# Hashed attention and a maxout feed-forward layer on one core: where operands are transposed, when weights are loaded, and how feed-forward work is spread over attention steps

## The chip, the cores and the metric

The kernel runs on one core of one Trainium2 chip. Its time is device time in microseconds (us) of one execution. Five engines take part, each working through its own instructions in order: PE (matmuls; PEld are its weight loads), DVE and ACT (element-wise work, the only two here that read PSUM), POOL (element-wise work in SBUF, and the issuing of most loads) and SP (only the issuing of transfers).

## The reference

```python
q_bits = (np.einsum('bhsd,dk->bhsk', q, proj) > 0).astype(np.int64)
k_bits = (np.einsum('bhsd,dk->bhsk', k, proj) > 0).astype(np.int64)
q_bucket = np.sum(q_bits * powers, axis=-1)      # powers = 1, 2, 4, ... 32
k_bucket = np.sum(k_bits * powers, axis=-1)
mask = q_bucket[:, :, :, None] == k_bucket[:, :, None, :]
scores = np.where(mask, scale * np.matmul(q, k.transpose(0, 1, 3, 2)), -1000000000.0)
attn = softmax(scores)                           # a row without a match becomes uniform
attn_out = np.matmul(attn, v)
x = attn_out.transpose(0, 2, 1, 3).reshape(B * S, H * D)
h = np.maximum(np.maximum(x @ w1, x @ w2), x @ w3)
out = h @ w_out
```

q, k and v are 4 x 8 x 768 x 64 (batch, heads, sequence, head size), proj is 64 x 6, w1 to w3 are 512 x 768, w_out is 768 x 512, the output 3072 x 512, all float32.

## The kernel before

**Attention.** Heads go in pairs: 4 batches of 4 pairs. For each pair, q and k are loaded as float32, split on DVE into an fp16 head (`tensor_scalar`, line 121) and an fp16 residual (line 122), and the result is transposed (line 125) by a DMA that SP issues, into `qT` and `kT` with 128 rows: 64 of heads, 64 of residuals. The hash is a matmul of all 128 rows with the projection (line 133, into `hps`, two halves of eight matmuls); DVE compares with zero (lines 144 and 150, `hb`) and writes six rows of plus or minus a constant over the first residual rows (line 154). Score matmuls then use 70 rows: scores plus a number that is largest where all six bits agree, so that the exponential of anything else vanishes. `vcast` makes fp16 v with a column of ones in `vone`; `meanv` gives the mean of v (`svp`, `mv`) for rows without a match.

**Units.** A unit is two blocks of 128 keys against 384 queries: 2 matmuls (line 186, `sc`), one ACT exponential of 128 x 768 (line 190, `AT`), 6 matmuls with v (line 206, `av`). There are 192 units: 4 batches, 2 halves of the queries, 4 pairs, 2 heads, 3 units. After the six units of a pair and half, `norm` divides by the sum (DVE lines 221, 223, 228; POOL 224, 225, 230) into `xn`.

**Feed-forward.** After the four pairs of a half batch, `xn` (384 tokens x 512) is transposed by one DMA that SP issues (line 233, `xT`). `push_ffn` appends 21 pieces called atoms: 18 first-layer atoms of 4 matmuls (line 246, `ps`; the first of three is copied by ACT on line 251, the others are maxed in by DVE on line 253, `ht`) with a cost of 0.64, and 3 output atoms of 6 matmuls (line 258, `po`; copied to `osb` by DVE or ACT, stored by SP) with a cost of 1.28.

**Order.** The order on every engine is that of the code. One step of the main loop issues the scores of unit u, the v matmuls of unit u-2, what the table `todo` holds for step u (loads, splits, hashes, means, put there by `at(step, ...)`), and atoms. From step 32 on each step adds a rate of about 0.76 to a credit, whether atoms are there or not, and issues atoms while the credit allows. Hashes, means and atoms share the PSUM pool `mm_ps`, which has two buffers.

**Loads.** The first q, k and v are issued by SP; the weights are four whole loads on POOL at steps 0, 1, 3 and 8; pairs of later batches are loaded by POOL 6 steps ahead of their split, and hashed 6 and 7 steps behind it, one pair every 5 steps.

Of the kernel before, what the change touches and what calls it, by code (L numbers as in the profile page):

```python
# [7 lines left out]

# [7 lines left out]
def kernel(  # L16
# [30 lines left out]
    TINY = 1e-30  # L47
# [39 lines left out]
    nc.vector.memset(bias_t[:], EXP_BIAS)  # L87
    ones = konst.tile([P, P], FP16, name="ones")
# [13 lines left out]
    nc.vector.tensor_copy(ph[:], p32[:])  # L102
# [7 lines left out]
    def load_w(i):  # L110
        w_ap = (moe_w1, moe_w2, moe_w3)[i]
        nc.gpsimd.dma_start(w_sb[i][:], w_ap.rearrange("(c p) f -> p c f", p=P))


    T = {}

    def split(b, pr):
        for n in "qk":
            x32 = raws.pop((n, b, pr))[:].rearrange("p h (c d) -> p (h c) d", d=D)
            s = spl.tile([P, 2 * NCH, 2 * D], FP16, tag=n + "s", name=n + "s")  # L120
# [7 lines left out]
    def hash_mm(b, pr, half):  # L128
        hps = mm_ps.tile([P, 512], FP32, tag="mm", name="hps")
        c0 = half * CH  # L130
        for s, w in ((True, PA), (False, PB)):
            for g, (n, hh) in enumerate((("q", 0), ("k", 0), ("q", 1), ("k", 1))):
                nc.tensor.matmul(hps[32 * g : 32 * (g + 1), 0:HQ], w[:],  # L133
                                 T[n, b, pr][:, hh * NCH + c0 : hh * NCH + c0 + CH, :],
                                 start=s, stop=not s)
        return hps

    hbs = {}

    def hash_a(b, pr):  # L140
# [190 lines left out]
    for u in range(N + LAG):  # L331
        if u < N:
            score(u)
        if u >= LAG:
            attend(u - LAG)
# [40 lines left out]
```

## Time and profile before

| | |
|---|---|
| median of 3 runs | 429.3 us (427.68 to 432.57) |
| profiled execution | 430.04 us |
| its span, first to last instruction | 428.2 us |
| busy in the span: PE, DVE, ACT, POOL | 301.5, 197.3, 190.2, 113.5 us |
| mean granted TensorE clock | 0.86 |

In the profile's rows a group reads: line, engine, operation, output <- inputs with the program's names, count, busy time and mean ns; behind the bar the idle time just before these instructions and what ended most of it. A row of the waits reads: who waited, for whom, us in total, times, longest. A row of the timeline reads: start, duration (us), engine, line and operation. The granted clock is a share of full speed.

### The profile page before, as it was taken

To read this page: it belongs to the slowest core of one execution; us is meant where nothing else is said; L and a number is where in the kernel's file an instruction comes from. 1 tells how busy PE (TensorE), PEld (TensorE's weight loads), DVE (VectorE), ACT (ScalarE), POOL (GpSimd) and SP (SyncE) were. 2 spreads that over 40 slices of the span, in tenths; PEclk is the share of its full clock that TensorE was granted. 3 is DMA by queue.
4 is the path that set the end of the run, shared out by engine and by line. 5 is a ranking of instruction groups with operands and counts; after the bars stand their busy time and mean duration, and the time that the engine had idled before them with its cause. 6 is when DMAs were issued, how large, how long until landed. Compare 5 with 4: busy or idle time off the path is not lost.

```text
span 428.2 us, 6629 instructions
## 1 busy us (share of the span) xinstructions
PE 301.5 (70%) x2608; PEld 174.0 (41%) x2608; DVE 197.3 (46%) x394; ACT 190.2 (44%) x249; POOL 113.5 (26%) x159
## 2 busy tenths in 40 slices
PE   0406785887979916886589915979649983998396
PEld 0103443453546613543346502545325552555152
DVE  4506538586525522977424431686614320431043
ACT  1204456352667723543527820445331693159210
POOL 1501249331113640421301670043210141004200
PEclk9999658596999976989979965998758997999689
DMA  7996957973030493473110594147510101010201
GB/s 239 244 222 142 149 148 182 214 196 73 2 110 2 138 287 93 100 159 100 57 29 2 184 219 112 35 112 187 75 37 0 51 26 37 2 73 3 38 0 73
DMA packets 75551, 44.47 MB, mean 104 GB/s; under 512 B 64096, under 2 KB 69328, under 8 KB 75520
## 3 DMA queue, kind: packets, MB, share of 16 engines
q1 hardware_dynamic: 68624, 25.57, 27.0%
q0 software_dynamic: 6736, 18.48, 16.2%
q8 instruction: 20, 0.33, 0.3%
q14 instruction: 11, 0.09, 0.1%
q10 hardware_dynamic: 160, 0.00, 0.0%
HBM read 25.17 MB, written 6.29 MB: 73 GB/s over the span
## 4 chain that ended last, share of the span: by engine, by line
PE 47%; DMA 21%; DVE 13%; ACT 8%; issue 4%; POOL 3%; SPq 2%; POOLq 0%; ACTq 0%; DVEq 0%
PE ps L246 24%; DMA kT<-ks 11%; PE sc L186 9%; DMA xT<-xn 8%; ACT AT L190 8%; PE po L258 6%; PE av L206 4%; PE hps L133 3%; DVE qs L122 3%; SPq L125 2%; DVE qs L121 2%; DVE ks L121 2%; DVE ht L253 1%; DMA v<-in_v_dram 1%; POOL xn L230 1%
## 5 line engine op out<-in xcount | busy, mean ns | idle before, releaser
L190 ACT ACTIVATE AT<-sc,bias_t 128x768 f16<-128x768 f32 x192 | 165.2, 908 | 117.6 <-PE sc L186 116.6
L246 PE MATMUL ps<-xT,w_sb 128*128 128x384 f16 x576 | 125.4, 361 | 54.9 <-DMA xT<-xn 52.9
L186 PE MATMUL sc<-qT,kT 70*128 70x384 f16 x384 | 104.7, 358 | 9.4 <-ACT AT L190 2.3
L253 DVE TENSOR_TENSOR ht<-ht,ps 128x384 f16<-128x384 f16 x96 | 53.1, 553 | 117.0 <-PE ps L246 114.1
L246 PEld LDWEIGHTS <-w_sb 128*128 128x128 f16 x576 | 56.8, 106 | 103.2 <-issue 67.7
L206 PEld LDWEIGHTS <-AT 128*128 128x128 f16 x1152 | 66.7, 103 | 32.4 <-issue 10.3
L224 POOL TENSOR_SCALAR m<-dd 128x6 f32<-128x6 f32 x32 | 7.1, 223 | 264.3 <-DVE dd L221 264.2
L206 PE MATMUL av<-vone,AT 128*128 128x65 f16 x1152 | 72.1, 201 | 0.6 <-ACT AT L190 0.4
L251 ACT CAST ht<-ps 128x384 f16<-128x384 f32 x48 | 22.9, 476 | 103.0 <-PE ps L246 103.0
L186 PEld LDWEIGHTS <-kT 70*128 70x128 f16 x384 | 36.3, 103 | 37.6 <-issue 22.3
L133 PE MATMUL hps<-qT,PA 128*32 128x384 f16 x64 | 16.5, 400 | 47.9 <-DMA qT<-qs 35.2
L258 PE MATMUL po<-wout_sb,ht 128*128 128x512 f16 x144 | 35.6, 385 | 0.5 <-DVE ht L253 0.4
L230 POOL TENSOR_TENSOR xn<-xn,t 128x384 f16<-128x384 f16 x32 | 30.5, 952 | 2.5
L133 PEld LDWEIGHTS <-PA 128*32 128x32 f16 x128 | 5.2, 98 | 60.2 <-issue 47.0
L225 POOL TENSOR_TENSOR t<-m,mv 128x384 f32<-128x384 f32 x32 | 26.5, 828 | 2.7
L221 DVE TENSOR_SCALAR dd<-av 128x6 f32<-128x6 f32 x32 | 5.2, 163 | 39.0 <-PE av L206 38.8
L144 DVE TENSOR_SCALAR hb<-hps 128x384 f16<-128x384 f32 x16 | 8.8, 551 | 29.9 <-PE hps L133 29.9
L159 POOL CAST vone<-v 128x768 f16<-128x768 f32 x16 | 17.7, 1104 | 16.7 <-DMA v<-in_v_dram 16.5
L264 DVE COPY osb<-po 128x512 f32<-128x512 f32 x16 | 11.0, 690 | 22.9 <-PE po L258 22.9
L122 DVE SCALAR_TENSOR_TENSOR qs<-q,qs 128x768 f16<-128x768 f32 x16 | 20.4, 1277 | 0.5
L258 PEld LDWEIGHTS <-ht 128*128 128x128 f16 x144 | 12.9, 99 | 14.4 <-issue 1.8
L133 PE MATMUL hps<-kT,PA 128*32 128x384 f16 x64 | 13.1, 399 | 7.8 <-DMA kT<-ks 7.8
(34 smaller groups left out, 192.2 us busy)
## 6 DMA issues: line engine op xcount, KB each, us to landing
out_dram<-osb SPq DMA_DIRECT2D x24, 256.0 KB, 2.0
v<-in_v_dram POOLq DMA_DIRECT2D x15, 384.0 KB, 6.7
q<-in_q_dram POOLq DMA_DIRECT2D x12, 384.0 KB, 3.9
k<-in_k_dram POOLq DMA_DIRECT2D x12, 384.0 KB, 5.3
w_sb<-in_moe_w_dram POOLq DMA_DIRECT2D x3, 768.0 KB, 12.8
q<-in_q_dram SPq DMA_DIRECT2D x4, 384.0 KB, 4.1
k<-in_k_dram SPq DMA_DIRECT2D x4, 384.0 KB, 6.0
wout_sb<-in_moe_w_out_dram POOLq DMA_DIRECT2D x1, 768.0 KB, 8.5
```

What stands on the lines that cost most here:

```text
L122: nc.vector.scalar_tensor_tensor(out=s[:, :, D : 2 * D], in0=x32, scalar=QS, in1=s[:, :, 0:D], op0=AluOp.mult, op1=AluOp.subtract)
L133: nc.tensor.matmul(hps[32 * g : 32 * (g + 1), 0:HQ], w[:], T[n, b, pr][:, hh * NCH + c0 : hh * NCH + c0 + CH, :], start=s, stop=not s)
L159: nc.gpsimd.tensor_copy(vones[b % 2][:, 2 * pr : 2 * pr + 2, :, 0:D], v32)
L186: nc.tensor.matmul(sc[:, i, 0:HQ], kT[0:KR, hh * NCH + 2 * j + i, :], qT[0:KR, hh * NCH + hf * CH : hh * NCH + (hf + 1) * CH, :], start=Tr ...
L190: nc.scalar.activation(AT[:], sc[:, :, 0:HQ], ActFn.Exp, bias=bias_t[:], scale=EXP_SCALE)
L206: nc.tensor.matmul(av[:, o : o + D + 1], AT[:, i, c * P : (c + 1) * P], vones[b % 2][:, 2 * pr + hh, 2 * j + i, 0 : D + 1], start=first, s ...
L225: nc.gpsimd.tensor_tensor(out=t[:], in0=m[:].to_broadcast([P, 2, CH, D]), in1=mvs[b, pr][:].unsqueeze(2).to_broadcast([P, 2, CH, D]), op=A ...
L230: nc.gpsimd.tensor_tensor(out=xv, in0=xv, in1=t[:], op=AluOp.add)
L246: nc.tensor.matmul(ps[:, 0:HQ], w_sb[i][:, jc, fb * P : (fb + 1) * P], xT[:, :, jc, :], start=jc == 0, stop=jc == NJ - 1)
L251: nc.scalar.copy(ht[:], ps[:, 0:HQ])
L253: nc.vector.tensor_tensor(out=hts[fb][:], in0=hts[fb][:], in1=ps[:, 0:HQ], op=AluOp.max)
L258: nc.tensor.matmul(ps[:], hts[fb][:, c * P : (c + 1) * P], wout_sb[:, fb, :], start=fb == 0, stop=fb == NF - 1)
```

## The change

1. **First pair.** Its q and k are loaded head by head, q by SP and k by ACT. The heads are split on DVE and ACT, and transposed on PE: `pe_T` issues six 128 x 128 transposes into a PSUM tile, `evac_T` copies it to `qT` or `kT` by DVE (q) or ACT (k). `hash_head` hashes one head at a time. The projection operands are made behind the first copy (`make_p`).
2. **Second pair.** Its halves are split by POOL and DVE, and transposed on PE as well, at step 2 (`second`).
3. **x.** After every pair `x_T` transposes its 384 x 128 part of x on PE, five steps after the pair's last unit; DVE copies it into `xT`. No DMA transposes x any more.
4. **Other pairs** are still transposed by DMA, 9 or 10 steps ahead of their hash, with loads 10 steps ahead of the split, one pair every 6 steps (second batch) or 10 (third and fourth).
5. **Weights** w1 to w3 are loaded in halves of their columns at steps 6, 7, 9, 12, 13, 14, w_out at step 18.
6. **Pace.** A step adds 0.64 to the credit, and only while atoms are there; 21 atoms cost 24 x 0.64, and a half batch has 24 units.
7. **Normalisation.** The mean of v, now with the column of ones and times 1e-30, is added to numerator and denominator, then one reciprocal and one product (POOL, or DVE for the last pair) follow.

The core of the diff:

```diff
-    load_qk(0, 0, nc.sync)
-    load_qk(0, 1, nc.sync)
-    load_v(0, 0, nc.sync)
+    load("q", 0, 0, nc.sync, (1, 2))
+    load("k", 0, 0, nc.scalar, (1, 2))
+    load("q", 0, 1, nc.sync)
+    load("k", 0, 1, nc.sync)
+    load("v", 0, 0, nc.gpsimd)
...
+    def pe_T(n, b, pr, hh, tag):
+        pool = av_ps if tag == "av" else mm_ps
+        ps = pool.tile([P, 512], FP32, tag=tag, name="tps")
+        p16 = ps[:].bitcast(FP16)
+        for c in range(NCH):
+            nc.tensor.transpose(p16[:, c * P : (c + 1) * P], S16[n, b, pr][:, hh * NCH + c, :], iden[:])
+        return p16
...
+    def hash_head(b, pr, hh):
+        tq, tk = T["q", b, pr], T["k", b, pr]
+        hb = small.tile([P, S], FP16, tag="hb", name="hb")
+        hps = hash_mm([(tk, hh, 0), (tq, hh, 0), (tk, hh, 1), (tq, hh, 1)])
+        hash_cmp(hb[:, 0:HQ], hps)
+        for g, (t, half) in enumerate(((tk, 0), (tq, 0), (tk, 1), (tq, 1))):
+            a = hh * NCH + half * CH
+            hash_row(t[D : D + NBITS, a : a + CH, :].rearrange("p a t -> p (a t)"),
+                     hb[32 * g : 32 * g + NBITS, 0:HQ])
...
             norm(b, hf, pr)
+            at(u + LAG + 3, lambda: x_T(b, hf, pr))
...
+        nc.vector.tensor_tensor(out=t[:, :, :, 0 : D + 1], in0=av[:, :, :, 0 : D + 1],
+                                in1=mvs[b, pr][:].unsqueeze(2).to_broadcast([P, 2, CH, D + 1]),
+                                op=AluOp.add)
+        nc.vector.reciprocal(rr[:], t[:, :, :, D : D + 1])
+        eng = nc.vector if pr == NP - 1 else nc.gpsimd
+        eng.tensor_tensor(out=xv, in0=t[:, :, :, 0:D], in1=rr[:].to_broadcast([P, 2, CH, D]),
+                          op=AluOp.mult)
+
+    def x_T(b, hf, pr):
         if pr == 0:
-            xns[b, hf] = xp.tile([P, CH, DM], FP16, tag="xn", name="xn")
...
+            xTs[b, hf] = xp.tile([P, NJ, HQ], FP16, tag="xT", name="xT")
+        xn = xns.pop((b, hf, pr))
+        ps = mm_ps.tile([P, 512], FP32, tag="mm", name="xps")
+        p16 = ps[:].bitcast(FP16)
+        for c in range(CH):
+            nc.tensor.transpose(p16[:, c * P : (c + 1) * P], xn[:, c, :], iden[:])
+        nc.vector.tensor_copy(xTs[b, hf][:, pr, :], p16[:, 0:HQ])
         if pr == NP - 1:
-            xT = xp.tile([P, CH, NJ, P], FP16, tag="xT", name="xT")
-            nc.sync.dma_start_transpose(xT[:].rearrange("p c j t -> p (c j) t"),
-                                        xns.pop((b, hf))[:].rearrange("p c m -> p (c m)"))
-            push_ffn(b, hf, xT)
+            push_ffn(b, hf, xTs.pop((b, hf)))
...
+    at(0, first_b)
+    at(1, lambda: split_r("q", 0, 1))
+    at(1, lambda: split_r("k", 0, 1))
+    at(2, second)
...
+    at(4, lambda: third(2))
+    at(6, lambda: load_w(0, 0))
+    at(8, lambda: third(3))
+    at(10, lambda: hash_half(0, 2, 0))
+    at(15, lambda: hash_half(0, 3, 0))
...
+    def prep(b, pr, s, lead, lag):
+        at(s - lead, lambda: [load(n, b, pr, nc.gpsimd) for n in "qkv"])
...
+        at(s, split)
+        at(s + 2, lambda: vcast(b, pr))
+        at(s + lag, lambda: hash_half(b, pr, 0))
+        at(s + lag + 1, lambda: hash_half(b, pr, 1))
+        at(s + lag + 1, lambda: hash_rows(b, pr))
+        at(s + lag + 2, lambda: meanv(b, pr))
...
+            if b == 1:
+                prep(b, pr, 32 + 6 * pr, 10, 9)
+            else:
+                prep(b, pr, 2 * (b - 1) * NUG + 14 + 10 * pr, 10, 10)
...
-        if u >= first and u < N:
-            credit += rate
+        if atoms:
+            credit += 0.64
```

(`first_b` and `second` call `pe_T` and `evac_T` for the second head of the first pair and for the second pair; `third` splits a pair and issues its DMA transposes.)

On SP, from the program's start, the issues before were these (loads of the first batch, with the transposes of the first two pairs between them; the names are the tiles written and read):

```order
L71 DMA q_99<-in_q_dram 128x2x384
L71 DMA k_101<-in_k_dram 128x2x384
L71 DMA q_103<-in_q_dram 128x2x384
L71 DMA k_105<-in_k_dram 128x2x384
L76 DMA v_107<-in_v_dram 128x2x384
L125 DMA_TRANSPOSE qT<-qs 128x12x128
L125 DMA_TRANSPOSE kT<-ks 128x12x128
L71 DMA q_141<-in_q_dram 128x2x384
L71 DMA k_143<-in_k_dram 128x2x384
L125 DMA_TRANSPOSE qT<-qs 128x12x128
L125 DMA_TRANSPOSE kT<-ks 128x12x128
```

In the changed kernel SP starts with these:

```order
L78 DMA q_96<-in_q_dram 128x384 x2
L78 DMA q_105<-in_q_dram 128x2x384
L78 DMA k_107<-in_k_dram 128x2x384
L78 DMA q_184<-in_q_dram 128x2x384
L78 DMA k_186<-in_k_dram 128x2x384
L78 DMA q_240<-in_q_dram 128x2x384
L78 DMA k_242<-in_k_dram 128x2x384
L152 DMA_TRANSPOSE qT<-qs 128x12x128
L152 DMA_TRANSPOSE kT<-ks 128x12x128
```

The four transposes of the first two pairs are gone, and the first one left (the third pair's) stands behind all q and k loads of the first batch.

On PE, where the feed-forward work of the first half batch begins, the rows before were these (the last matmuls of a mean, then the first atom, which reads the `xT` that a DMA writes):

```order
L166 LDWEIGHTS ones
L166 MATMUL svp<-vone_115,ones 128x128
L246 LDWEIGHTS w_sb
L246 MATMUL ps<-xT,w_sb 128x384
L246 LDWEIGHTS w_sb
L246 MATMUL ps<-xT,w_sb 128x384
```

In the changed kernel the same place reads (last matmul with v, three transposes of the last pair's part of x, first atom):

```order
L261 MATMUL av<-vone_122,AT 128x65
L292 LDWEIGHTS xn
L292 MATMUL xps<-iden,xn 128x128
L292 LDWEIGHTS xn
L292 MATMUL xps<-iden,xn 128x128
L292 LDWEIGHTS xn
L292 MATMUL xps<-iden,xn 128x128
L306 LDWEIGHTS w_sb
L306 MATMUL ps<-xT,w_sb 128x384
```

PE now makes the transposed x itself, in the rows right ahead of the atom that needs its copy.

On DVE, where a pair of a later batch is split (heads and residuals of q and k) while the pair before it is hashed (`hb` are the two compares, then four writes of rows), the rows before were these:

```order
L121 TENSOR_SCALAR qs<-q_1967 128x12x64
L122 SCALAR_TENSOR_TENSOR qs<-q_1967,qs 128x12x64
L121 TENSOR_SCALAR ks<-k_1969 128x12x64
L122 SCALAR_TENSOR_TENSOR ks<-k_1969,ks 128x12x64
L144 TENSOR_SCALAR hb<-hps 128x384
L253 TENSOR_TENSOR ht<-ht,ps 128x384
L150 TENSOR_SCALAR hb<-hps 128x384
L154 TENSOR_SCALAR qT<-hb 6x768
```

In the changed kernel a pair of the third batch:

```order
L179 TENSOR_SCALAR hb<-hps 128x384
L142 TENSOR_SCALAR qs<-q_1853 128x12x64
L148 SCALAR_TENSOR_TENSOR qs<-q_1853,qs 128x12x64
L142 TENSOR_SCALAR ks<-k_1855 128x12x64
L148 SCALAR_TENSOR_TENSOR ks<-k_1855,ks 128x12x64
L293 COPY xT<-xps 128x384
L313 TENSOR_TENSOR ht<-ht,ps 128x384
L179 TENSOR_SCALAR hb<-hps 128x384
L183 TENSOR_SCALAR qT<-hb 6x768
```

The first compare has moved ahead of the split; the second stays behind it, now with a copy of x between. In the second batch of the changed kernel split and hash of different pairs lie three steps apart.

More of the change, by code (lines that the diff above doesn't have):

```diff
@@ L129, in hash_mm @@
+    def hash_mm(groups):
         hps = mm_ps.tile([P, 512], FP32, tag="mm", name="hps")
[L130 removed]
         for s, w in ((True, PA), (False, PB)):
[L132 to L134 removed]
+            for g, (t, hh, half) in enumerate(groups):
+                a = hh * NCH + half * CH
+                nc.tensor.matmul(hps[32 * g : 32 * (g + 1), 0:HQ], w[:], t[:, a : a + CH, :],
@@ L148, in hash_b, with hash_row, hash_half, hash_rows @@
+    def hash_row(dst, src):
+        nc.vector.tensor_scalar(out=dst, in0=src, scalar1=2 * BIT, scalar2=None, op0=AluOp.mult)
+    hbs = {}
+    def hash_half(b, pr, half):
+        if half == 0:
+            hbs[b, pr] = small.tile([P, S], FP16, tag="hb", name="hb")
+        tq, tk = T["q", b, pr], T["k", b, pr]
+        hps = hash_mm([(tq, 0, half), (tk, 0, half), (tq, 1, half), (tk, 1, half)])
+        hash_cmp(hbs[b, pr][:, half * HQ : (half + 1) * HQ], hps)
+    def hash_rows(b, pr):
         hb = hbs.pop((b, pr))
-        hps = hash_mm(b, pr, 1)
@@ new lines, with first_b, second @@
+    hash_head(0, 0, 0)
+    split_r("k", 0, 0, (1, 2))
+    vcast(0, 0)
+    for n in "qk":
+        load(n, 0, 2, nc.sync)
+    load("v", 0, 1, nc.gpsimd)
+    operands(0, 1)
+    split_h("q", 0, 1, nc.gpsimd)
+    split_h("k", 0, 1, nc.gpsimd)
+    def first_b():
+        pq = pe_T("q", 0, 0, 1, "mm")
+        pk = pe_T("k", 0, 0, 1, "mm")
+        evac_T(pq, "q", 0, 0, 1, nc.vector)
+        evac_T(pk, "k", 0, 0, 1, nc.scalar)
+        hash_head(0, 0, 1)
+    def second():
+        for n in "qk":
+            for hh in range(2):
+                ps = pe_T(n, 0, 1, hh, "mm")
+                evac_T(ps, n, 0, 1, hh, nc.vector if n == "q" else nc.scalar)
@@ new lines, in third @@
+    def third(pr):
+        operands(0, pr)
+        for n in "qk":
+            split_h(n, 0, pr, nc.gpsimd if pr == 2 else nc.vector)
+            split_r(n, 0, pr)
+            xbar(n, 0, pr)
+    at(0, first_b)
+    at(0, lambda: vcast(0, 1))
+    at(1, lambda: split_r("q", 0, 1))
+    at(1, lambda: split_r("k", 0, 1))
+    at(2, second)
+    at(1, lambda: [load(n, 0, 3, nc.sync) for n in "qk"])
+    at(1, lambda: load("v", 0, 2, nc.gpsimd))
+    at(3, lambda: load("v", 0, 3, nc.gpsimd))
+    at(3, lambda: hash_half(0, 1, 0))
@@ L326 @@
     N = len(units)
-    total = 2 * B * (18 * 0.64 + 3 * 1.28)
-    first = NUG + 8
-    rate = total / (N - first + 2)
     credit = 0.0
-    for u in range(N + LAG):
+    for u in range(N + LAG + 4):
         if u < N:
             score(u)
-        if u >= LAG:
+        if LAG <= u < N + LAG:
             attend(u - LAG)
```

208 lines of the change are left out of this document (109 added, 99 removed).

## The prediction

> **What bounds the kernel now.** I cut the span at four places of the program: the first score matmul, step 32 (the first feed-forward matmul stands there), the last score step, the end. The table of windows gives each engine's busy time (with its count of instructions), the granted TensorE clock, the DMA share and GB/s; two later windows lie where operands for the next batch are made.
>
> ```profile
> 0.00:16.60 16.60, 1.94 (x16) 0.69 (x16) 9.76 (x22) 1.28 (x1) 6.90 (x12) 1.00 0.88 232
> 16.60:81.60 65.00, 37.40 (x339) 21.60 (x340) 29.44 (x59) 26.62 (x32) 19.43 (x26) 0.80 0.86 184
> 81.60:398.30 316.70, 242.50 (x2164) 142.18 (x2164) 149.18 (x296) 158.88 (x210) 85.17 (x118) 0.87 0.35 87
> 398.30:428.20 29.90, 19.69 (x90) 9.52 (x89) 8.94 (x17) 3.45 (x7) 1.97 (x3) 0.81 0.14 40
> 170.00:210.00 40.00, 32.60 (x333) 19.04 (x331) 31.26 (x60) 20.92 (x28) 10.81 (x14) 0.96 0.45 110
> 270.00:310.00 40.00, 31.03 (x308) 17.62 (x307) 29.69 (x57) 18.98 (x24) 10.81 (x14) 0.89 0.51 110
> ```
>
> The first column of busy time is PE. It works 37.4 of 65.0 us in the second stage, while DMA is at 0.86 of its engines; in the third it works 242.5 of 316.7, with every other engine half idle and DMA at 0.35. So the question is what PE, which takes its instructions in order, waits for. The first row below is from the waits of the whole span, the other two from the third stage alone (us in total, times, longest).
>
> ```profile
> PE hps L133 <- DMA qT<-qs: 35.2, 6, 13.2
> ...
> PE ps L246 <- DMA xT<-xn: 46.7, 6, 13.7
> PE hps L133 <- DVE hb L144: 12.8, 6, 2.9
> ```
>
> In the early stages PE stands at the hash matmuls for operands transposed by DMA; in the third at the first feed-forward matmul of each half batch, for the DMA transposition of x. What it does when nothing holds it is in the timeline of PE (start, duration, instruction):
>
> ```profile
> 127.20 0.49 PE L186 MATMUL sc<-qT,kT 70*128 70x384 f16 x2
> 127.53 0.35 PE L206 MATMUL av<-vone,AT 128*128 128x65 f16 x6
> 127.71 0.81 PE L246 MATMUL ps<-xT,w_sb 128*128 128x384 f16 x4
> 128.36 0.49 PE L186 MATMUL sc<-qT,kT 70*128 70x384 f16 x2
> ```
>
> One step with one feed-forward atom takes 128.36 - 127.20 = 1.16 us; 0.65 of it is the atom (127.71 to 128.36). Without an atom ACT sets the pace, by two neighbours of the chain that ended last:
>
> ```profile
> 385.09 0.71 ACT AT L190
> 385.87 0.72 ACT AT L190
> ```
>
> 0.78 us a step. A long wait has a second price, which the windows around the last x transposition show: PE idles 5.40 us, then runs 24 matmuls in 7.00 us at a clock of 0.58, and only afterwards 48 in 8.60 at 1.00.
>
> ```profile
> 399.00:404.40 5.40, 0.00 (x0) 0.00 (x0) 0.37 (x1) 0.00 (x0) 1.69 (x2) 0.60 0.38 73
> 404.40:411.40 7.00, 6.91 (x24) 3.24 (x24) 1.65 (x3) 0.96 (x2) 0.00 (x0) 0.58 0.01 2
> 411.40:420.00 8.60, 8.54 (x48) 4.62 (x48) 4.30 (x9) 1.91 (x4) 0.00 (x0) 1.00 0.00 0
> ```
>
> At the later rate (0.18 each) the 24 would have taken 4.3 us, so the slow clock costs 2.7 us per restart.
>
> **The change, stage by stage.** I build the new span from the four stages. Step numbers are those of the loop over units.
>
> *To the first score (16.6 us now).*
>
> ```profile
> 5.88 0.17 DVE L102 CAST ph<-p 128x6 f16<-128x6 f32 x1 [4.40 <-DMA p<-in_proj_dram]
> ...
> 12.18 0.48 PE L133 MATMUL hps<-qT,PA 128*32 128x384 f16 x1 [12.18 <-DMA qT<-qs]
> ...
> 14.52 0.56 DVE L144 TENSOR_SCALAR hb<-hps 128x384 f16<-128x384 f32 x1 [1.03 <-PE hps L133]
> ...
> 16.63 1.46 PE L186 MATMUL sc<-qT,kT 70*128 70x384 f16 x4 [1.50 <-DVE kT L154]
> ```
>
> DVE now does nothing until the projection has landed at 5.88, and PE waits for qT until 12.18. The half loads of one head go out first and on two queues, so I let them land by 5.5. Then follow two residuals of half size (0.5 each), twelve transposes, copies out of PSUM of 768 columns (0.9, by the 908 ns of an ACT pass of that width below), the small projection operands (4 x 0.17), one hash instead of two (13.65 to 14.52 now, 0.9), compare 0.6, four half rows 0.8. Sum 5.5 + 1.2 + 0.8 + 0.9 + 0.7 + 0.9 + 0.6 + 0.8 = 11.4; call it **11**, bounds 10 to 14.
>
> *Steps 0 to 31 (65.0 us now).*
>
> ```profile
> 12.96 8.49 SPq L125 DMA_TRANSPOSE qT<-qs  x1
> ...
> 32.80 0.48 PE L133 MATMUL hps<-qT,PA 128*32 128x384 f16 x1 [13.23 <-DMA qT<-qs]
> ```
>
> The second pair's qT, issued at 12.96 behind loads on SP, releases PE at 32.80 after a wait of 13.23. This pair goes to PE now and its wait falls away. What is late next is the serial work of the new steps 0 to 4: step 0 transposes and hashes the second head (two copies, hash, compare, rows: 4 us), step 2 pushes four transposed heads through the two buffers of `mm_ps` (DVE and ACT copies in turn, 5), steps 3 and 4 hash (two rounds of 0.9 + 0.6, rows 4 x 0.35, 5). Thus step 5 comes at about 26. Steps 5 to 10 go at 0.78, to 30. Pairs 2 and 3 still come by DMA, issued at about 28 and 32 beside weight loads; with 8 to 12 us each (between the median of 5.3 of the page and the 20 us above) their hashes stand until 36 and 44; the rows are out at 47, step 18. Ten steps at 0.78 give 55, four with atoms and the first x transposes 62. So **51 us** for this stage; at least 35 (28 steps at 0.78, 4 at 1.16, 8 of serial work), at most the 65 of now.
>
> *Steps 32 to 191 (316.7 us now).* An atom of 0.64 credit per step and a group worth 24 x 0.64 make one atom (or half an output atom of 1.3) each step: 160 x 1.16 = 185.6. To this PE adds 24 half hashes, 12 means and 27 transpositions of x (three matmuls each):
>
> ```profile
> 274.87 0.96 DVE L122 SCALAR_TENSOR_TENSOR qs<-q,qs 128x768 f16<-128x768 f32 x1
> ...
> 275.13 0.34 PE L133 MATMUL hps<-qT,PA 128*32 128x384 f16 x1
> ...
> 275.57 0.44 PEld L246 LDWEIGHTS <-w_sb 128*128 128x128 f16 x4 [0.32 <-issue]
> ...
> 283.37 0.50 PE L166 MATMUL svp<-vone,ones 128*128 128x128 f16 x6
> ...
> 283.71 0.49 PE L186 MATMUL sc<-qT,kT 70*128 70x384 f16 x2
> ```
>
> A half hash is 275.57 - 275.13 = 0.44 (24 make 10.6), a mean 283.71 - 283.37 = 0.34 (12: 4.1). A 128x128 transpose on PE is not in the trace. Its nearest row is one matmul of the mean, 0.34 / 6 = 0.057; from above I bound it by that group's mean latency, unpipelined:
>
> ```profile
> L166 PE MATMUL svp<-vone,ones 128*128 128x128 f16 x96 | 9.3, 241 | 1.6 <-DVE hb L144 1.6
> ```
>
> 0.057 x 81 = 4.6 us, at most 0.241 x 81 = 20. I take 4.6, since independent transposes follow each other as those six do. PE work: 185.6 + 10.6 + 4.1 + 4.6 = 205. The Trainium skill speaks against this choice: "TensorE: Matmul & The Clock Gate", Part 4 (PE-mode transpose), gives about 275 ns for one in a kernel and says that the full clock does not engage for it. By that the term would be an estimated 22 us; no run here shows either.
>
> Now the stalls. A prep (splitting q and k of a pair) holds DVE for 0.55 + 0.96 + 0.55 + 0.96 = 3.0 us when undisturbed, while copies out of PSUM queue behind it and PE has only two buffers to fill. Three rows of now:
>
> ```profile
> 277.81 0.32 PE L133 MATMUL hps<-qT,PA 128*32 128x384 f16 x1 [0.90 <-DVE hb L144]
> ...
> 281.05 0.81 PE L246 MATMUL ps<-xT,w_sb 128*128 128x384 f16 x4 [0.80 <-DVE ht L253]
> ...
> 285.32 1.46 DVE L122 SCALAR_TENSOR_TENSOR qs<-q,qs 128x768 f16<-128x768 f32 x1
> ...
> 289.44 0.32 PE L133 MATMUL hps<-qT,PA 128*32 128x384 f16 x1 [2.70 <-DVE hb L144]
> ```
>
> One pair cost 0.90 + 0.80, another 2.70; the two windows of 40 us hold eight pairs and 7.4 + 9.0 us of idle PE, 2.05 a pair. For the second batch the hashes now stand three or more steps away from a split; for the third and fourth the first compare stands ahead of the split and the second still behind it. I take 2.5 per pair (what a clock drop adds included), 12 x 2.5 = 30, between 1.0 and 5.4 (2.7 and one clock restart of 2.7). A transposition of x takes one of the two buffers and its copy goes through DVE: 0.3 x 27 = 8.1, an estimate from the 0.55 of such a copy less the room that the second buffer gives. The first atom of each group needs the copy that stands right ahead of it: 0.8 x 6 = 4.8. What goes is the wait of 46.7 and the slow clock behind it; what is late next is DVE. Sum 205 + 30 + 8.1 + 4.8 = **248 us**; bounds 217 (12 x 1.0, nothing else) and 300 (12 x 5.4, transposes at 0.241).
>
> One more rule of the skill bears on the splits that POOL now does for two pairs beside DVE's residuals: "SBUF — State Buffer", Who interferes with whom, says that a DVE instruction with two SBUF inputs blocks against a GpSimd one that reads SBUF. The residual is such an instruction, and the trace agrees that it is not always 0.96: 1.46 at 285.32, where POOL was issuing loads (whether that reads SBUF no row shows). For four residuals that is an estimated 2 us, inside the bounds of the second stage.
>
> The normalisation trades two DVE and three POOL instructions for others of that size, with DVE at 149 of 316.7: nothing on the path. The loads of later pairs go out ten steps ahead on POOL; DMA is at 0.35 there, which hides them; without that cover they are the fourth rival. Weight halves and the output queue cost nothing for the same reason.
>
> *From the last score step (29.9 us now).* x no longer waits for POOL and DMA (398.3 to 404.5), and the clock stays up.
>
> ```profile
> 424.28 0.69 DVE L264 COPY osb<-po 128x512 f32<-128x512 f32 x1 [1.90 <-PE po L258]
> ```
>
> Left are some 2.6 us of the seventh group, 18 atoms at 8.60 / 12 = 0.72 (13), three output atoms 4, and 428.2 - 424.28 = 3.9 for the last copy and its store: **24**.
>
> Sum: 11 + 51 + 248 + 24 = 334 us of span. The profiled execution took 430.04 with a span of 428.2, so 1.8 lie outside, and it stands 0.2% above the median of 429.3. **336 us**.
>
> **The rivals.** (1) *DVE becomes the bound of the third stage*: each pair stalls PE for 2.7 us and drops the clock, 5.4 a pair. For it: 289.44. Against it: 0.96 and 0.89 as the clock of the two windows, so most stalls do not drop it. 336 + 12 x 2.9 = 371. (2) *The early stage stays bound by transfers*: pairs 2 and 3 each hold PE like the second pair now, 13 us, and the stage stays near its 65. For it: DMA at 0.86; against it: two pairs' transpositions leave it and the weights come later. 336 + 14 = 350. (3) *Transposes on PE do not pipeline*, 0.241 each for 81 + 48 of them: 336 + 129 x 0.184 = 360. For it: nothing but that mean; against it: the six matmuls of a mean in 0.34. The rule of "TensorE: Matmul & The Clock Gate" quoted above is this case, at an estimated 364. (4) *Slower than before*: PE stands at the hash of every later pair for its DMA transposition, as it does at 32.80. Split and first hash lie 9 or 10 steps apart, some 13 us at 1.16 and a little. To lose all of the gain and 4 us more, 98 us over 12 pairs, every transposition must come 8 us later than that, 21 after its split; the 20 us of the second pair is the one such case, at a DMA share of 0.86, and the third stage has 0.35. It would give 434 and more. (5) *The change does not even the pace*: PE and ACT alternate as before, the start gains nothing, and only the waits for x go. 428.2 less 46.7, less seven clock restarts (19) and 6 in the tail, is 356, with 1.8 outside 358. For it: PE holds the same atoms; against it: the credit now runs only while atoms wait.
>
> **How the numbers follow.** The forecast, 312 to 349: 0.60. Rival 1, 355 to 380: 0.14. Rival 2: 0.10. Rival 3: 0.05. Rival 5: 0.04. Fewer stalls than I count, below 312: 0.04. Rival 4: 0.02; between it and the others 0.01. The range of 312 to 371 holds the forecast, rivals 2, 3 and 5 and half of 1, 0.86 One per cent, 4 us, is about what a measurement of this kernel tells from no change. Faster by more than that 0.97, within it 0.01, slower 0.02.
>
> **What would show it.** First score near 11 and step 32 near 62; no wait of PE for xT by DMA; one step with an atom at 1.16 still; granted clock of the third stage above 0.95; longest total wait of PE put down to DVE. I am wrong if hash matmuls wait for qT or kT after step 32, if the three transposes of x take much over 0.2 us, or if steps between preps are longer than 1.16.

## The result and the profile after

The changed kernel takes 360.5 us (median of four runs, 358.4 to 361.6) where the kernel before takes 430.6 on the same chip: a ratio of 0.837, with a 95% interval of 0.831 to 0.844. The forecast was 336 with a range of 312 to 371. The direction and the range held; the time came out 24 us above the forecast, and outside the 312 to 349 to which the forecast itself had given 0.60.

The profiled execution has a span of 359.8 us. The table of windows of the changed kernel, cut at the same four places of the program (columns as before: length, busy time of PE, PEld, DVE, ACT and POOL, the granted clock, the DMA share, GB/s):

```profile
0.00:13.90 13.90, 2.33 (x21) 1.58 (x22) 5.78 (x19) 3.52 (x6) 6.28 (x11) 1.00 0.75 255
13.90:76.50 62.60, 44.89 (x389) 28.02 (x389) 28.19 (x57) 30.74 (x36) 22.36 (x24) 0.70 0.81 133
76.50:335.10 258.60, 224.34 (x2230) 138.29 (x2229) 157.33 (x313) 158.96 (x208) 51.88 (x63) 0.95 0.42 102
335.10:359.80 24.70, 20.39 (x118) 10.30 (x116) 10.90 (x20) 4.05 (x8) 0.00 (x0) 1.00 0.17 64
```

| stage | before | forecast | measured | off by |
|---|---|---|---|---|
| to the first score | 16.6 | 11 | 13.9 | +2.9 |
| steps 0 to 31 | 65.0 | 51 | 62.6 | +11.6 |
| steps 32 to 191 | 316.7 | 248 | 258.6 | +10.6 |
| from the last score step | 29.9 | 24 | 24.7 | +0.7 |

58 of the 68 us that the span lost came out of the third stage; the forecast had 69 of 94 there. The second stage kept nearly all of its length. What PE waited for in the whole span (total us, times, longest):

```profile
PE ps L306 <- DVE ht L313: 12.2, 9, 2.8
PE hps L174 <- DMA kT<-ks: 10.1, 2, 8.7
PE xps L292 <- DVE ht L313: 9.2, 5, 2.2
```

No wait for xT by DMA is left. The longest single wait, 8.7 us, is still one for an operand transposed by DMA; the largest total is DVE's.

**The second stage.** The chain that ended last has one long transfer, and the timeline of PE shows the hash that stood for it, that of the fourth pair. The third row is POOL's issue of weight halves, which went out just ahead of the transposition:

```profile
36.86 17.69 DMA kT<-ks
```
```profile
54.59 0.48 PE L174 MATMUL hps<-kT,PA 128*32 128x384 f16 x1 [8.69 <-DMA kT<-ks]
```
```profile
35.34 1.54 POOL L124 DMA_DIRECT2D w_sb<-in_moe_w_dram  x2
```

The transposition was issued at 36.86 and landed 17.7 us later, beside the weights. Windows of the same kernel behind that show a second thing:

```profile
36.00:55.00 19.00, 8.42 (x72) 4.76 (x71) 4.67 (x11) 4.50 (x5) 4.04 (x6) 0.51 1.37 134
55.00:70.00 15.00, 14.97 (x126) 9.35 (x120) 5.60 (x14) 10.58 (x12) 5.17 (x7) 0.50 0.76 179
```

From 55 to 70 PE is busy throughout, and yet its clock stays at 0.50; in this kernel it is up again only behind the first feed-forward atoms (rows of 70.64 and 74.15 in the last section).

**The third stage.** The timeline of PE, with and without a transposition of x:

```profile
324.41 0.49 PE L241 MATMUL sc<-qT,kT 70*128 70x384 f16 x2
324.74 0.35 PE L261 MATMUL av<-vone,AT 128*128 128x65 f16 x6
324.92 0.33 PE L292 MATMUL xps<-iden,xn 128*128 128x128 f16 x3
325.29 0.81 PE L306 MATMUL ps<-xT,w_sb 128*128 128x384 f16 x4
325.94 0.49 PE L241 MATMUL sc<-qT,kT 70*128 70x384 f16 x2
326.26 0.35 PE L261 MATMUL av<-vone,AT 128*128 128x65 f16 x6
326.45 0.81 PE L306 MATMUL ps<-xT,w_sb 128*128 128x384 f16 x4
327.10 0.49 PE L241 MATMUL sc<-qT,kT 70*128 70x384 f16 x2
```

A step with an atom is 327.10 - 325.94 = 1.16 us, as before. With three transposes of x it is 325.94 - 324.41 = 1.53, so the three cost 0.37. What PE stands for at a prep, on DVE:

```profile
183.84 0.93 DVE L142 TENSOR_SCALAR qs<-q 128x768 f16<-128x768 f32 x1
184.81 0.96 DVE L148 SCALAR_TENSOR_TENSOR qs<-q,qs 128x768 f16<-128x768 f32 x1
185.68 0.56 DVE L142 TENSOR_SCALAR ks<-k 128x768 f16<-128x768 f32 x1
186.27 0.96 DVE L148 SCALAR_TENSOR_TENSOR ks<-k,ks 128x768 f16<-128x768 f32 x1
187.15 0.55 DVE L179 TENSOR_SCALAR hb<-hps 128x384 f16<-128x384 f32 x1
...
189.21 0.55 DVE L313 TENSOR_TENSOR ht<-ht,ps 128x384 f16<-128x384 f16 x1
```

and on PE:

```profile
184.51 0.34 PE L174 MATMUL hps<-qT,PA 128*32 128x384 f16 x1
...
187.75 0.51 PE L221 MATMUL svp<-vone,ones 128*128 128x130 f16 x6 [1.46 <-DVE hb L179]
189.82 0.33 PE L292 MATMUL xps<-iden,xn 128*128 128x128 f16 x3 [1.56 <-DVE ht L313]
```

The hash ran on PE at 184.51; its compare came on DVE at 187.15, behind the four splits of the next pair (183.84 to 187.23, 3.4 us). Then four hash rows follow, and only after them, at 189.21, what an atom's buffer waits for. Two windows show the clock behind such a pair of waits:

```profile
188.00:192.00 4.00, 2.44 (x18) 1.41 (x16) 2.81 (x8) 0.00 (x0) 0.00 (x0) 0.77 1.10 220
192.00:196.00 4.00, 4.00 (x32) 2.06 (x30) 1.30 (x3) 2.18 (x3) 0.00 (x0) 0.80 0.58 134
```

### The profile page after: what moved, and what is told of

Same layout as the page of the kernel before. It is cut to its first block, busy times and chain, and to the rows that moved or that the text cites. A ratio compares the mean times of both kernels' runs of the same rounds, so it can differ in the third digit from the quotient of the medians.

```text
span 359.8 us, 6801 instructions
## 1 busy us (share of the span) xinstructions
PE 292.0 (81%) x2752; PEld 178.2 (50%) x2752; DVE 202.2 (56%) x407; ACT 197.3 (55%) x257; POOL 80.5 (22%) x97
## 4 chain that ended last, share of the span: by engine, by line
PE 62%; DVE 24%; DMA 8%; issue 4%; ACT 1%; ACTq 0%; DVEq 0%
PE ps L306 24%; PE sc L241 15%; PE av L261 8%; PE po L318 8%; DMA kT<-ks 6%; DVE qs L148 4%; PE hps L174 4%; DVE ht L313 3%; DVE hb L179 3%; DVE ks L142 2%; DVE qT L183 2%; DVE qs L142 2%; DMA k<-in_k_dram 2%; DVE kT L183 2%; DVE ks L148 2%
## 5 line engine op out<-in xcount | busy, mean ns | idle before, releaser
L245 ACT ACTIVATE AT<-sc,bias_t 128x768 f16<-128x768 f32 x192 | 171.5, 903 | 103.4 <-PE sc L241 102.0
L306 PE MATMUL ps<-xT,w_sb 128*128 128x384 f16 x576 | 121.3, 337 | 14.0 <-DVE ht L313 12.2
L282 POOL TENSOR_TENSOR xn<-t,rr 128x384 f16<-128x384 f32 x24 | 20.8, 868 | 242.4 <-PE sc L241 139.0
L306 PEld LDWEIGHTS <-w_sb 128*128 128x128 f16 x576 | 50.4, 100 | 46.8 <-issue 26.8
L311 ACT CAST ht<-ps 128x384 f16<-128x384 f32 x48 | 22.8, 475 | 33.2 <-PE ps L306 33.2
L179 DVE TENSOR_SCALAR hb<-hps 128x384 f16<-128x384 f32 x32 | 17.7, 554 | 34.3 <-PE hps L174 34.2
L174 PE MATMUL hps<-kT,PA 128*32 128x384 f16 x64 | 12.3, 377 | 15.7 <-DMA kT<-ks 10.1
L277 DVE TENSOR_TENSOR t<-av,mv 128x390 f32<-128x390 f32 x32 | 18.0, 561 | 6.1 <-PE av L261 5.8
L174 PE MATMUL hps<-qT,PA 128*32 128x384 f16 x64 | 13.2, 378 | 7.5 <-DVE xT L293 4.2
L292 PE MATMUL xps<-iden,xn 128*128 128x128 f16 x96 | 11.5, 234 | 9.2 <-DVE ht L313 9.2
L213 POOL CAST vone<-v 128x768 f16<-128x768 f32 x16 | 16.6, 1042 | 6.5 <-DMA v<-in_v_dram 6.3
L148 DVE SCALAR_TENSOR_TENSOR qs<-q,qs 128x768 f16<-128x768 f32 (+1 forms) x17 | 17.5, 1031 | 0.5
L148 DVE SCALAR_TENSOR_TENSOR ks<-k,ks 128x768 f16<-128x768 f32 (+1 forms) x17 | 17.0, 998 | 0.5
## 6 DMA issues: line engine op xcount, KB each, us to landing
w_sb<-in_moe_w_dram POOLq DMA_DIRECT2D x6, 384.0 KB, 11.6
```

The lines of the kernel that those rows point to most:

```text
L148: nc.vector.scalar_tensor_tensor(out=s[:, a, D : 2 * D], in0=x32, scalar=QS, in1=s[:, a, 0:D], op0=AluOp.mult, op1=AluOp.subtract)
L174: nc.tensor.matmul(hps[32 * g : 32 * (g + 1), 0:HQ], w[:], t[:, a : a + CH, :], start=s, stop=not s)
L179: nc.vector.tensor_scalar(out=out, in0=hps[:, 0:HQ], scalar1=0.0, scalar2=0.5, op0=AluOp.is_gt, op1=AluOp.subtract)
L245: nc.scalar.activation(AT[:], sc[:, :, 0:HQ], ActFn.Exp, bias=bias_t[:], scale=EXP_SCALE)
L277: nc.vector.tensor_tensor(out=t[:, :, :, 0 : D + 1], in0=av[:, :, :, 0 : D + 1], in1=mvs[b, pr][:].unsqueeze(2).to_broadcast([P, 2, CH, D ...
L282: eng.tensor_tensor(out=xv, in0=t[:, :, :, 0:D], in1=rr[:].to_broadcast([P, 2, CH, D]), op=AluOp.mult)
```

## The experiments

My theory after the result: the 24 us lie in two places, (A) the early transfers, which hold the fourth pair's hash and with it step 32 (76.5 against 62), and (B) preps that hold DVE in one piece for longer than the buffers ahead of PE last. Its rivals: the early stage is slow through its clock; the sum of DVE's work counts, not its grouping. (The expectations below letter their own theories and rivals.) Beside it four parts of the change are undone one at a time; the weight halves and the new normalisation were not. Ratios are to the kernel before on the same chip; the changed kernel was not timed again beside these runs, which are from three chips, so differences of a few us from its 360.5 are rough.

**spread.** The two halves of a prep three steps apart; the work is the same.

```diff
-        at(s, split)                      # both q and k
+        at(s, lambda: [operands(b, pr), split("q")])
+        at(s + 3, lambda: split("k"))
```

> The changed kernel with the same split work for the pairs of later batches, but q split at step s and k three steps later, so DVE is held in two blocks of about 1.5 us instead of one of 3.0 to 4.4. Theory A (PE loses time because one block on DVE is longer than the two PSUM buffers cover): waits of PE for DVE fall from about 33 us to under 18, time 342 to 352. Rival B (the sum of work on DVE matters, not its place): time within 3 us of 360. Rival C (k arrives later at its hash): waits of hash matmuls for kT after step 32, time over 362.

Measured: 335.2 us (334.5 to 337.0), 0.781 (0.775 to 0.788). The windows of this kernel, cut at its own step 32 and last score step:

```profile
13.00:75.30 62.30, 43.66 (x388) 27.38 (x388) 28.97 (x57) 30.59 (x36) 21.88 (x24) 0.73 0.82 134
75.30:309.20 233.90, 213.73 (x2230) 134.10 (x2228) 153.48 (x313) 158.66 (x208) 51.36 (x63) 1.00 0.47 112
```

The third stage falls from 258.6 to 233.9 with as many instructions and almost the same DVE time (153.5 for 157.3). Of the 24.7 us, 14.1 are idle PE time (258.60 - 224.34 = 34.3 becomes 20.2), and 10.6 are the same matmuls at a clock of 1.00 in place of 0.95 (224.34 to 213.73). PE's waits for DVE in this stage add up to 17.3 us where the changed kernel has 33.2, as expected; the two largest of those shown above, 12.2 and 9.2, become 8.5 and 3.2. So the grouping of DVE's work is the cause, by the waits and, for 10.6 us, by the slow clock that came with them. This is (B) above, the expectation's Theory A, and it is worth more than I gave it (335 for 342 to 352). Its Rival C shows as one wait of 1.8 us for kT behind step 32.

**act_heads.** The fp16 heads of later pairs by ACT in place of DVE, which also shortens the block on DVE.

```diff
-                split_h(n, b, pr, nc.vector)
+                split_h(n, b, pr, nc.scalar)
```

> The changed kernel with the fp16 heads of later batches made by ACT instead of DVE (24 instructions of 0.9 us move from DVE to ACT). Theory A (DVE block): the block falls from 3.0 to 1.9 us, the waits of PE for DVE to under 22 us, time 344 to 353. Rival B (ACT, whose exponentials queue behind two passes of 0.9 us, becomes what PE waits for): waits of score matmuls for ACT appear, time 358 or more.

Measured: 351.8 us (350.9 to 352.9), 0.819 (0.813 to 0.826). The block is shorter but still in one piece, and DVE now also stands ahead of it for the head that ACT makes (12.6 us in 12 waits). PE's waits for DVE in the third stage fall to 25 us, not under 22; the gain is 8.7 us where the spreading gave 25.

**late_w.** The first halves of the weights at steps 15 to 17, the second at 20 to 23.

```diff
-    at(6, lambda: load_w(0, 0))
...
-    at(12, lambda: load_w(0, 1))
...
+    at(15, lambda: load_w(0, 0))
...
+    at(20, lambda: load_w(0, 1))
```

> The changed kernel with its weight loads behind the hash of the fourth pair: first halves at steps 15, 16, 17, second halves at 20, 21, 23, w_out at 26. Theory A (the weight loads delay the DMA transposes of the fourth pair, whose kT took 17.7 us to land): the wait of PE at that hash falls from 8.7 us to under 2, kT lands in under 8 us, and the time falls from 360 to 349 to 354. Rival B (four transposes in a row on SP are slow by themselves): the wait stays over 6 us and the time within 3 us of 360. If the first feed-forward atoms must then wait for weights, PE shows a wait at line 306 near step 28.

Measured: 354.8 us (353.4 to 358.2), 0.829 (0.819 to 0.839). That is slightly above the 349 to 354 expected. The fourth pair's hash no longer stands for 8.7 us (its kT, issued at 38.69, is there when PE reaches the hash at 45.70), and step 32 comes at about 62, the place that I had forecast; but in this kernel's chain another transposition has taken the place of that one, and one row of PE waits for it:

```profile
66.64 17.39 DMA kT<-ks
```
```profile
84.08 0.32 PE L174 MATMUL hps<-kT,PA 128*32 128x384 f16 x1 [3.37 <-DMA kT<-ks]
```

Theory A holds as to the cause. Of the 14 us by which step 32 is earlier, only 8 are left in the profiled span (359.8 to 351.7), and 5.7 by the medians: the weights now run beside the operands of the second batch.

**spread_late.** Both, with the weights at steps 14 to 20.

```diff
+    at(14, lambda: load_w(0, 0))
...
+    at(18, lambda: load_w(0, 1))
```

> Both improvements together: q and k split three steps apart, and the weight loads behind the hash of the fourth pair (first halves at steps 14, 15, 16, second halves at 18, 19, 20, w_out at 24). If the two losses are separate ones: 335 less 6 to 14, so 321 to 330. If the transfers only move into the transposes of the second batch: 331 to 337, with waits of hash matmuls for kT of 3 us or more near steps 41 to 53.

Inconclusive: four executions took 326.1, 349.4, 344.3 and 346.9 us, too far apart for a comparison. Only the first, which would fit the first branch, has a trace, so what took the 20 us in the others stays open.

**fill.** Four wide matmuls that nothing needs, at each of steps 17 to 19, to see whether they bring the early clock up.

```diff
+    for s in (17, 18, 19):
+        at(s, fill)          # 4 matmuls of 128 rows, 384 columns
```

> The changed kernel with four more matmuls of 384 columns over all 128 rows in each of steps 17, 18 and 19 (their result is not used), where PE runs score and value matmuls at half clock. If it is the kind of matmul that keeps the clock low there (70 rows, or 65 columns), the granted clock rises within two windows of these steps, near 65 us instead of 74, and steps 22 to 28 take 0.8 us each instead of 0.97. If the clock is low for another reason, it rises at about the same distance behind the first feed-forward atoms as now, and the time is 3 to 5 us longer.

One execution, 357.6 us. The granted clock reads 1.00 in the whole early stage of this trace, but the matmuls themselves are slow there: the six value matmuls of a unit take 0.54 us until the fill and 0.35 behind it, as they do in the changed kernel at clocks of 0.50 and 1.00.

```profile
55.69 0.54 PE L261 MATMUL av<-vone,AT 128*128 128x65 f16 x6
56.04 1.47 PE L422 MATMUL fps<-vone,ones 128*128 128x384 f16 x4
...
59.48 0.35 PE L261 MATMUL av<-vone,AT 128*128 128x65 f16 x6
```

So the record of the clock has a gap here. (The changed kernel's has it too: 1.00 from 13.9 to 25 us, where the value matmuls take 0.54; in the third stages compared above their lengths agree with it.) And the rate did rise, within 2.1 us of the first wide group (at 58.16 a mean runs at its full rate), nine us ahead of the first feed-forward atom at 67.28; steps then follow at 0.79 where the changed kernel has 0.97. That fits the first branch. But such matmuls are not needed for it. In late_w the value matmuls take 0.54 at 45.24 and 0.35 at 48.37, 9.6 us before the first matmul of that width (128 rows, 384 columns, 128 results). With one execution, and late_w against it, the kind of matmul is not shown to be the cause, and why the clock stays down for 15 us under a busy PE remains open. The wait for the fourth pair's kT was 4.3 us here, although the program is the changed kernel's up to that point (8.7), so this wait differs between executions.

What the early clock is worth can be read from late_w, where most of this stretch ran at the full rate: from the first kT matmul of the fourth pair's hash to the first feed-forward matmul it takes 45.70 to 57.99, 12.3 us, and the changed kernel takes 54.59 to 70.64, 16.1. That is some 4 of the 14.5 us by which step 32 is late, so the clock rival carries a part, and the wait the larger one. The mean clock of whole executions does not settle it: those of spread (0.949, 0.942, 0.998 and 0.998, at 335.7, 337.0, 334.5 and 334.8 us) may have the same gap as the record of fill.

**early_pe.** spread, and the third and fourth pair also transposed on PE, so that no transposition by DMA is left ahead of step 32. The weights stay where they were.

```diff
     for n in "qk":
...
         split_r(n, 0, pr)
-        xbar(n, 0, pr)
...
+    at(8, lambda: third_T(2, "q"))     # pe_T and evac_T of both heads
+    at(9, lambda: third_T(2, "k"))
+    at(13, lambda: third_T(3, "q"))
+    at(14, lambda: third_T(3, "k"))
```

> The changed kernel with q and k of later batches split three steps apart (as in the run of that name) and the third and fourth pair of the first batch transposed on PE too, so that no DMA transpose runs beside the weight loads. The wait of 8.7 us at the fourth pair's hash and the slow clock behind it go; PE gets 48 more transposes of about 0.06 to 0.12 us and DVE and ACT four copies each. Expected: step 32 at 58 to 64 us instead of 75, time 318 to 327; if the copies through two buffers cost as much as the DMA did: 332 to 338.

Measured: 323.0 us (320.1 to 323.8), 0.748 (0.743 to 0.754): the fastest of all, faster than both kernels compared. Its second stage:

```profile
13.90:60.60 46.70, 36.52 (x436) 24.85 (x436) 29.67 (x62) 32.36 (x40) 22.50 (x24) 1.00 0.70 145
```

The second stage falls from 62.3 (spread) to 46.7 us with the same weights at the same steps, and step 32 comes at 60.6, as expected. Two ways of taking the transposition and the weights apart, late_w and this one, both remove the wait; only this one leaves PE no wait for a DMA anywhere in the span.

**early_pe_act.** The same with the heads by ACT.

```diff
-            split_h(n, b, pr, nc.vector)
+            split_h(n, b, pr, nc.scalar)
```

> The same with the fp16 heads of later batches made by ACT. If DVE still holds PE: 3 to 8 us less than the run without it. If ACT has become as late as DVE: the same or up to 4 us more.

Measured: 333.8 us (333.3 to 334.9), 0.775 (0.771 to 0.779), 11 us slower than early_pe. The rival had the direction, though not the size (at most 4). The waits of DVE in this kernel:

```profile
DVE qs L148 <- ACT qs L140: 11.7, 11, 2.1
DVE ks L148 <- ACT ks L140: 11.1, 10, 2.7
```

DVE, in order, stands at 21 of the 24 residuals for the head that ACT makes behind its exponentials. That with the split spread there was no long block left for ACT to shorten is my reading; no run separates it.

Four kernels undo one part of the change each.

**first_dma.** The first two pairs transposed by DMA again.

```diff
-    pq = pe_T("q", 0, 0, 0, "av")
...
+        xbar(n, 0, 0)
...
-    at(0, first_b)
...
-    at(2, second)
```

> The changed kernel with its first two pairs split on DVE and transposed by DMA as in the kernel before, all else as changed. If transposing them on PE is what shortened the start: first score at 16 to 17 instead of 13.9, hash of the second pair 5 to 13 us late, time 368 to 378. If the early stage is bound by the transposes of the later pairs anyway: time 358 to 364.

Measured: 360.2 us (359.2 to 363.0), 0.841 (0.834 to 0.848): the same as the changed kernel, as in the second branch. Its first score step, later than either branch had it, and its hash of the fourth pair:

```profile
20.61 1.46 PE L241 MATMUL sc<-qT,kT 70*128 70x384 f16 x4 [1.42 <-DVE kT L183]
```
```profile
52.23 0.48 PE L174 MATMUL hps<-kT,PA 128*32 128x384 f16 x1 [3.06 <-DMA kT<-ks]
```

The units begin 6.7 us later (13.86 becomes 20.61), and the fourth pair's hash comes 2.4 us earlier (52.23 for 54.59). In the changed kernel the early start ended in the wait for the fourth pair. Whether it pays once that wait is gone, as in late_w and early_pe, no run shows: both have the first two pairs on PE.

**x_dma and x_dma_now.** x transposed by one DMA per half batch, as before the change; its atoms become available at the changed kernel's step (three steps after the half batch ends), or at once.

```diff
+            nc.sync.dma_start_transpose(xT[:].rearrange("p c j t -> p (c j) t"),
+                                        xns.pop((b, hf))[:].rearrange("p c m -> p (c m)"))
...
# x_dma_now only, the push right behind that issue:
-            at(u + LAG + 3, lambda: x_T(b, hf, pr))
+            push_ffn(b, hf, xT)
```

> The changed kernel with x transposed by one DMA per half batch again, issued when the last pair is normalised, the atoms pushed at the same step as in the changed kernel. If transposing x on PE is where most of the gain of the third stage comes from: PE waits for xT by DMA again, 3 to 8 us at each of 8 places plus a slow clock behind, time 380 to 410. If the even pace is what gained: 355 to 370, with waits for xT under 2 us each.

> The changed kernel with x transposed by one DMA per half batch and the atoms pushed at once behind that issue, as in the kernel before; the pace stays even. Theory D (what saved the waits for x is the distance of three steps between the end of a half batch and its first atom, not the engine that transposes): PE waits for xT by DMA again, 5 to 8 us at 8 places, 40 to 55 us in total, time 392 to 412. Rival (the even pace alone hides the transposition): waits under 20 us, time 362 to 372.

Measured: 365.5 us (364.3 to 366.4), 0.851 (0.844 to 0.858), and 402.3 (400.2 to 405.8), 0.932 (0.925 to 0.939). The waits for xT, of the first and of the second:

```profile
PE ps L303 <- DMA xT<-xn: 15.1, 8, 5.8
```
```profile
PE ps L298 <- DMA xT<-xn: 49.0, 8, 9.1
```

The wait that the change was seen to remove (52.9 in the whole span before, 46.7 of it in the third stage) is back nearly in full when the atoms are pushed at once. With the DMA kept and three steps left to it, the kernel is 5 us slower than with PE, and most waits are 0.6 to 1.8 us, the first 5.8 and the last 2.9. So of the 42 us between x_dma_now and the changed kernel, some 37 belong to the distance and 5 to the engine (35 and 6 by the ratios, as the two ran on different chips).

**old_pace.** Credit by the former rate, and from the former first step.

```diff
-        if atoms:
-            credit += 0.64
+        if u >= first and u < N:
+            credit += rate
```

> The changed kernel with the pace of before: from step 32 a credit of about 0.76 a step, whether atoms wait or not. Theory P (the even pace is the main source of the gain of the third stage, since x by DMA again cost only 5 us): atoms come in bursts behind each push, ACT stands during them and PE waits for nothing but ACT in between, time 378 to 395. Rival (what gained is only that PE no longer stands idle for x, the pace does not matter): 358 to 366.

Measured: 382.5 us (382.1 to 384.6), 0.893 (0.886 to 0.900): the even pace is worth 22. The time is the theory's; that PE waits for ACT in between its bursts is not what the trace names, which puts 3.4 us of PE's waits in the third stage down to ACT, 23.4 to DVE and 6.1 to DMA, so how the pace gains is not shown.

**old_prep.** Preps of later batches every five steps, their loads six steps ahead and hashes six behind.

```diff
-            if b == 1:
-                prep(b, pr, 32 + 6 * pr, 10, 9)
...
+            prep(b, pr, (2 * b - 1) * NUG - 2 + 5 * pr, 6, 6)
```

> The changed kernel with the pairs of later batches prepared as before: one every 5 steps, loads 6 steps ahead of the split, hash 6 and 7 steps behind it, the last half batch of each batch without any. If the wider spacing carries part of the gain: hash matmuls wait for qT or kT and for compares that stand behind a split, 8 to 20 us more, time 368 to 380. If the waits only move with the splits: 357 to 364.

Measured: 371.0 us (369.0 to 375.9), 0.859 (0.853 to 0.866), 9 to 10 slower. With six steps, hashes wait for DMA again (the traced execution is the longest of the four):

```profile
PE hps L174 <- DMA kT<-ks: 22.6, 6, 9.8
PE hps L174 <- DMA qT<-qs: 6.0, 3, 3.1
```

Of these 28.6 us, 9.2 are of the first batch, where the changed kernel stood 12.0; the other 19.3 are of later batches, where it has none, and half of them is the one wait of 9.8, at the first hash of the second batch. How large they are in the other three executions is not known.

Undone alone, the parts cost 42 (distance and PE for x), 22 (pace), 10 (preps) and 0 (first pairs), 74 together against a gain of 70, so they do not simply add up.

## Why the prediction was right, and where it was off

The direction came, and most of the gain from the third stage, as worked out. The number did not: 360.5 stands next to rival 1's 355 to 380, rival 3's 360 and rival 5's 358, but only the first of these is there in part, as the paragraphs below show; that the other two lie so near is chance. What is too long is the early stage, which is rival 2, and PE's own work in the third. Of the signs named, three came: no wait for xT by DMA, the step of 1.16, and DVE as the largest total; the first score (13.9 for 11), step 32 (76.5 for 62) and the clock (0.95, not above) did not, and one sign of being wrong did: the three transposes of x take 0.37 us, not some 0.2.

**To the first score, 11 forecast, 13.9 measured.** I let the half loads land by 5.5 us (and put two residuals of 0.5 into the sum as 1.2), and missed what stood on ACT. The copy of kT that the first hash needs was queued behind ACT's split of the second head, and that waited for a later load:

```profile
9.96 0.52 ACT L140 ACTIVATE ks<-k 128x384 f16<-128x384 f32 x1 [4.63 <-DMA k<-in_k_dram]
10.39 0.78 ACT L165 COPY kT<-tps 128x768 f16<-128x768 f16 x1
```

The step that failed is the one that costs a chain by its own operations without the queue of the engine that carries them. That queue is not all of it: the projection landed at 8.85, not at 5.88, and the last of its operands (DVE, 9.99, 0.17 us) was ready at 10.16, so without the wait on ACT the hash at 11.22 would have come about 1 us earlier. By first_dma it is also a term that the total did not feel.

**Steps 0 to 31, 51 forecast, 62.6 measured.** The serial work of the first steps was sized well (step 5 at 27.3 for 26, the third pair's hash at 36.3 for 36). The term "8 to 12 us each" for the transposes of pairs 2 and 3 was wrong for one of them: 17.7, so that the fourth hash stood until 54.6 and not until 44. That is 10.6 of the 14.5 us by which step 32 is late (54.59 for 44); late_w and early_pe, which take weights and transposition apart, bring step 32 to 62 and 60.6. The stage is rival 2's, through one pair and not two. I had put that rival (13 us each, 350 us) at 0.10 with both numbers in view, DMA at 0.86 and the 20 us of the second pair, and argued that the weights come later; two weight halves went out at 35.34 all the same, 1.5 us ahead of the transposition. The other 3.9 us are the following steps, at the slow clock: late_w takes 3.8 less for them.

**Steps 32 to 191, 248 forecast, 258.6 measured.** The step of 1.16 held. Two terms were off. PE's own work came to 213.7 at full clock (spread), against the 205 of the sum: the transposes of x cost 0.37 per half pair and not 0.17, which makes 27 x 0.20 = 5.4 of it; the other 3.3 I have not traced. The stalls, 43 in the sum (30 for preps, 8.1 and 4.8 for x), came to 34.3 of idle PE and 10.6 of slow clock, 45 together: the sum was right, and the mechanism (DVE, with clock drops) was the one named. Whether its three terms were right is not shown: spread takes away 24.7 and leaves 20.2 idle. That more than half of it could be undone by moving the instructions of a split alone I had not asked. Rival 1 at 5.4 us a pair was too dear: 45 over 12 pairs is 3.7 with the x copies in it.

**The tail, 24 forecast, 24.7 measured**, for the reasons given.

**Rival 3, transposes that do not pipeline at 0.241.** Not so. The second pair, at half the rate (the score matmuls at 24.36 take 0.84 where those at 27.32 take 0.50; the granted clock reads 1.00 there, the same gap as in fill):

```profile
21.66 1.46 PE L159 MATMUL tps<-iden,qs 128*128 128x128 f16 x12 [2.27 <-DVE qs L148]
```

Twelve in 1.46 us are 0.122 each, and three with their gap 0.37 at the clock of the third stage. "TensorE: Matmul & The Clock Gate" of the Trainium skill, Part 4 (PE-mode transpose), gave some 275 ns for one. As a latency no run here contradicts that; as a price per transpose in a group, these rows are less than half of it. Its other half, that such transposes do not bring the clock up, was not separated here.

**Rival 4, slower**, did not come: the third stage of the changed kernel has no wait for DMA; old_prep shows that with six steps such waits are there (9.8 us at most); where between six and nine they begin was not run. **Rival 5**: the pace is evened, and worth 22 us (old_pace).

**POOL beside DVE.** The Trainium skill's "SBUF — State Buffer", Who interferes with whom, made me allow 2 us for four residuals, within the bounds. What was slow in the trace is rather POOL's split itself, and small DVE operations beside it:

```profile
10.63 2.14 POOL L142 TENSOR_SCALAR qs<-q 128x768 f16<-128x768 f32 x1
```
```profile
13.04 0.76 DVE L183 TENSOR_SCALAR qT<-hb 6x384 f16<-6x384 f16 x1
13.84 0.25 DVE L183 TENSOR_SCALAR kT<-hb 6x384 f16<-6x384 f16 x1
```

The same hash row takes 0.76 in the one place and 0.25 in the other, both beside a POOL split (the second of these ran from 12.85 for 2.19 us). These rows have one input, not two; the section also counts one-input operations in a two-port mode as blocked, which 0.76 would fit and 0.25 would not. Which of the two ran in such a mode no row shows, and no run here isolates it.

## What to carry to other kernels

Where a matmul engine works in order behind a few PSUM buffers, look at how long the engine that empties them is held in one piece, not at its busy share: the same DVE work in two pieces three steps apart was worth 25 us of 360, 10.6 of it at a faster clock. Give a slow transfer distance before giving it another engine: three steps between the transposition and its first reader were worth some 37 us, the engine 5. An early start is worth nothing while a slow transfer of the same stage still stands behind it: transposes on PE gained 0 for the first two pairs, and 12 us for the next two on top of them.

## What the runs showed that I had not expected

- The granted clock stayed at 0.50 for 15 us of a fully busy PE (55 to 70 us, mostly score and value matmuls) and was up within 3.5 us of the first feed-forward matmuls, as the last two rows below show (a score matmul takes 0.49 again). "TensorE: Matmul & The Clock Gate", Part 1, in the Trainium skill says that about 3.4 us of sustained busy time release the clock; the 15 us do not agree with that. In late_w the rate was back after 6 us of a busy PE (41.06 to 47.08) with no feed-forward matmul. It costs some 4 us here.

```profile
69.37 0.83 PE L241 MATMUL sc<-qT,kT 70*128 70x384 f16 x2
70.64 1.49 PE L306 MATMUL ps<-xT,w_sb 128*128 128x384 f16 x4
...
74.15 0.49 PE L241 MATMUL sc<-qT,kT 70*128 70x384 f16 x2
```

- Two waits of 1.5 us close together (ending at 187.75 and 189.82), no longer, were followed by clocks of 0.77 and 0.80 in two windows of 4 us.
- The transposition of one pair's kT from SBUF to SBUF took 4.3 us at 32.03 (the third pair), and 17.7 at 36.86 (the fourth), five microseconds later, beside the weight loads:

```profile
32.03 4.27 DMA kT<-ks
```
